# Decode attention with MLP on one core: last V tile in halves, slot addresses on 256-byte boundaries, early w2 rows, four stores

## Chip, cores and metric

One core of one Trainium2 chip. The metric is device time in microseconds (us) of an execution; medians of several runs are quoted. A profile adds one execution with a timeline; its span is about 1.5 us shorter than the timed number of the same kernel.

## The reference, cut to what matters

Batch 4, one query token, 32 heads of 128, a K and a V cache of 4096 positions: 8 MB for every tile (8 heads of one batch), 16 tiles of K and 16 of V, so 268 MB that are read once. Around them stand small projections.

```python
q = (layernorm(x) @ wq)                         # 4 x 640 -> 32 heads x 128
p = softmax(einsum("bhqd,bhkd->bhqk", q, k_cache) * Dh**-0.5)
h = x + einsum("bhqk,bhkd->bhqd", p, v_cache).reshape(4, 1, 4096) @ wo
t = layernorm(h) @ w1 + b1                      # 640 -> 1728
out = h + (t * tanh(softplus(t))) @ w2          # 1728 -> 640
```

## The kernel before

Three slots of 64 KB per partition take the K and V tiles. At the end wo and w1 come into slot B and w2 into slot A. One queue (SyncE) issues nearly all loads, in the order of this listing. TensorE does Q.K by folding products that VectorE made, then P.V, and in the tail a chain of small steps. `need` means "wait for"; the mark `("F", i, s)` says that part s of Q.K of tile i is folded, `("PV", i)` that P.V of tile i is done.

```python
SB0, SLOT0 = 16512, 229344 - 3 * SLOT * 2       # SLOT0 = 32736: 224 bytes past a multiple of 256
slot = {c: nc.alloc_sbuf_tensor_at(f"slot{c}", (P, SLOT), BF16,
        offset=SLOT0 + k * SLOT * 2).ap() for k, c in enumerate("ABC")}
...
def v_load(i):
    c = VS[i % N]
    load(sp, slot[c][:, :], tiles(A_v_cache, i), ("V", i), "V" + c)   # 128 rows of 64 KB
...
def sync_prog():
    ...                                          # K and V tiles; V of tile 15 is the last
    sp.need(("F", NT - 1, NS - 1))
    for q in range(NHG):                         # wo in four quarters of 1.3 MB
        load(sp, wo_sb[:, q, :, :], ..., ("wo", q), f"W{q}")
    for k, (c0, c1) in enumerate(zip(W1S, W1S[1:])):   # w1 in chunks 0-2 and 3-4
        load(sp, w1_sb[:, c0:c1, :], ..., ("w1", c0), f"W{NHG + k}")
    sp.need(("PV", NT - 2))
    load(sp, w2_tail[0:FT, :], B_w2[FM * P : F, :], "w2t", "WT")      # 64 rows, 80 KB
    for k, (j0, j1) in enumerate(zip(W2S, W2S[1:])):   # w2 in three parts
        load(sp, w2_sb[:, j0:j1, :], ..., ("w2", j0), f"W{NHG + 2 + k}")
    store(sp, 0); leave(sp, 0)                   # the other half of out goes by ScalarE's queue
...
def pv_mm(i):
    pe.need(("e", i, NS - 1), ("V", i))          # e: masked exponentials
    for u in range(nu):                          # 64 matmuls
        mm(pv[k * QD : (k + 1) * QD, :], e[...], t[:, u * 512 : (u + 1) * 512], ...)
...
def pe_tail():
    wo_mm(0); o_mm(NT - 1); l_mm(hg); wo_mm(1); a_mm(hg)   # wo_mm(k) needs wo quarter k and heads k
    ...
    wo_mm(2); wo_mm(3)
    ...                                          # layer norm, w1, mish, w2, o_bf
```

The softmax here doesn't subtract the row's maximum and nothing guards it: scores larger than these inputs give would overflow.

Of the kernel before, what the change touches and what calls it, by code (L numbers as in the profile page):

```python
# [14 lines left out]
class Prog:  # L15
# [38 lines left out]
    def do(self, fn, mark=None, sem=None, by=1):  # L54
# [5 lines left out]
                ins.then_inc(self.book.handles[sem], by)  # L60
        return ins


class Book:
    def __init__(self):
# [7 lines left out]
def kernel(  # L73
# [13 lines left out]
    nc = tc.nc  # L87
# [26 lines left out]

    book = Book()
    WSEM = ["WQ", "WT"] + [f"W{k}" for k in range(9)]
    for s in ["PE", "DV", "DVP", "DVA", "AC", "ACP", "PO", "KA", "KB", "VA", "VC", "X", "S", "OUT0", "OUT1", "FIN"] + WSEM:
        book.handles[s] = nc.alloc_semaphore(s)

    SB0, SLOT0 = 16512, 229344 - 3 * SLOT * 2  # L120
    at = [SB0]

    def sb(name, shape, dt, region=at, top=SLOT0):
# [17 lines left out]
    s_f = sb("s_f", (P, R), FP32)  # L141
    ex = sb("ex", (P, R), BF16)
    e = sb("e", (P, R, G), BF16)
    pv_sb = sb("pv_sb", (P, RQ, Dh), FP32)
    SW = 2 * BG - G
    selo = sb("selo", (P, RQ, SW), FP32)
    om = sb("om", (BG, G, Dh), BF16)
    rs = sb("rs", (P, N, NS), FP32)
    rs1 = sb("rs1", (P, N), FP32)
    rsm = sb("rsm", (P, N, G), FP32)  # L150
# [6 lines left out]
    delta = sb("delta", (BG, N), BF16)  # L157
    a_t = sb("a_t", (P, NHG, G, N), BF16)
    b1T = sb("b1T", (P, FC), BF16)
    eps = sb("eps", (P, 1), FP32)  # L160
    ones = sb("ones", (P, 1), FP32)

# [18 lines left out]
    w2_sb = slot["A"][:, 0 : FM * D].rearrange("p (j n) -> p j n", n=D)  # L181
    tail = [sA + FM * D * 2]
    topA = sA + SLOT * 2
    w2_tail = sb("w2_tail", (P, D), BF16, tail, topA)
    ones_d = sb("ones_d", (P, P), FP32, tail, topA)
    ident_f = sb("ident_f", (P, P), FP32, tail, topA)
    zeros = sb("zeros", (P, OC), BF16, tail, topA)
# [5 lines left out]
    std2 = sb("std2", (P, N), FP32, tail, topA)  # L193
    rstd = sb("rstd", (P, N), FP32, tail, topA)
    b1s = sb("b1s", (P, FC, N), FP32, tail, topA)
    ROW = QD // N
    spread = sb("spread", (P, 2 * DC + FC, N, ROW), BF16, tail, topA)
    h_hi, h_lo, act = (
        spread[:, j0:j1, :, :] for j0, j1 in ((0, DC), (DC, 2 * DC), (2 * DC, 2 * DC + FC))
    )  # L200
    h1 = sb("h1", (P, FC, N), FP32, tail, topA)
    ta = sb("ta", (P, FC, N), FP32, tail, topA)
    tb = sb("tb", (P, FC, N), FP32, tail, topA)
# [30 lines left out]
    po = Prog(nc.gpsimd, book)  # L234
    ac = Prog(nc.scalar, book)
    dv = Prog(nc.vector, book)
    pe = Prog(nc.tensor, book, take=["DVP", "DVA", "ACP", "VA", "VC"] + WSEM)

    def tiles(src, i):
        hg, b = divmod(i, N)  # L240
# [2 lines left out]
    def load(p, dst, src, key, sem):  # L243
        p.do(lambda: p.eng.dma_start(out=dst, in_=src), key, sem, 16)

    def store(p, h):
        c, n = CG // 2, D // 2
        p.need("o_bf")
        load(
            p, out_rows[:, h * n : (h + 1) * n].rearrange("b (k o) -> k b o", k=c),  # L250
            o_bf[h * P // 2 : (h + 1) * P // 2 : ROW, :], ("out", h), f"OUT{h}",
        )

    def leave(p, h):
        fin, o = book.handles["FIN"], book.handles[f"OUT{h}"]
        if p.live:
            p.eng.sem_inc(fin, 1)
            p.eng.wait_ge(o, 16).then_inc(o, -16)

    def clear():  # L260
        fin = book.handles["FIN"]
# [8 lines left out]

    def v_load(i):
        c = VS[i % N]
        load(sp, slot[c][:, :], tiles(A_v_cache, i), ("V", i), "V" + c)

    def first_loads():
        load(
            sp, slot["C"][:, 0 : DC * H * Dh], A_wq.rearrange("(p c) n -> p (c n)", c=DC), "wq", "WQ"
        )
        load(ac, x_bf[:, :], x_rows[:, :], "x", "X")
        k_load(0)  # L280
        k_load(1)

    def sync_prog():
        for hg in range(NHG):
            i = hg * N
            if hg:
                sp.need(("PV", i - 2))
                k_load(i)
                sp.need(("F", i - 1, NS - 1))
                k_load(i + 1)  # L290
            sp.need(("PV", i - 1) if hg else ("qb", NHG - 1))
            v_load(i)
            sp.need(("F", i, NS - 1))
            k_load(i + 2)
            sp.need(("PV", i))
            v_load(i + 1)
            sp.need(("F", i + 1, NS - 1))
            k_load(i + 3)
            sp.need(("F", i + 2, NS - 1))
            v_load(i + 2)  # L300
            sp.need(("PV", i + 1))
            v_load(i + 3)
        sp.need(("F", NT - 1, NS - 1))
        for q in range(NHG):
            load(
                sp, wo_sb[:, q, :, :],
                A_wo[q * QN : (q + 1) * QN, :].rearrange("(p j) n -> p j n", j=G), ("wo", q), f"W{q}",
            )
        w1_v = B_w1.rearrange("(p c) n -> p c n", c=DC)
        for k, (c0, c1) in enumerate(zip(W1S, W1S[1:])):  # L310
            load(sp, w1_sb[:, c0:c1, :], w1_v[:, c0:c1, :], ("w1", c0), f"W{NHG + k}")
        sp.need(("PV", NT - 2))
        load(sp, w2_tail[0:FT, :], B_w2[FM * P : F, :], "w2t", "WT")
        w2_v = B_w2[0 : FM * P, :].rearrange("(p j) n -> p j n", j=FM)
        for k, (j0, j1) in enumerate(zip(W2S, W2S[1:])):
            load(sp, w2_sb[:, j0:j1, :], w2_v[:, j0:j1, :], ("w2", j0), f"W{NHG + 2 + k}")
        store(sp, 0)
        leave(sp, 0)

    def pool_prog():  # L320
        g = nc.gpsimd
        po.do(lambda: g.memset(ident[:, :], 0.0), "id0", "PO")
        po.need("id0")
        po.do(
            lambda: g.affine_select(
                out=ident[:, :], in_=ident[:, :], compare_op=ALU.not_equal, fill=1.0, base=0,
                pattern=[[-1, P]], channel_multiplier=1,
            ),
            "ident", "PO",
        )  # L330
        po.do(lambda: g.memset(b1T[:, :], 0.0), "b1z", "PO")
        po.do(lambda: g.memset(lnT[:, :, :], 0.0), "lnz", "PO")
        po.do(lambda: g.memset(sel[:, :, :], 0.0), "selz", "PO")
        po.do(lambda: g.memset(selo[:, :, :], 0.0), "seloz", "PO")
        po.do(lambda: g.memset(ones[:, :], 1.0), "ones", "PO")
        po.need(("PV", NT - 2))
        po.do(lambda: g.memset(ones_d[:, :], 1.0 / D), "ones_d", "PO")
        po.do(lambda: g.memset(spread[:, :, :, :], 0.0), "spread", "PO")
        po.do(lambda: g.memset(zeros[:, :], 0.0), "zeros", "PO")
        po.do(lambda: g.tensor_copy(out=ident_f[:, :], in_=ident[:, :]), "ident_f", "PO")  # L340

# [80 lines left out]
    def dve_prog():  # L422
# [153 lines left out]
        for i in range(NT):  # L576
            hg, b = divmod(i, N)
            mult(i, 0)
            mult(i, 1)
            reduce(i, 0)  # L580
            mult(i, 2)
            if b == 0 and hg:
                norm(hg - 1)
            elif b == 0:
                dv.do(lambda: v.memset(om[:, :, :], 0.0), ("om", -1), DVP)
            reduce(i, 1)
            mult(i, 3)
            reduce(i, 2)
            if b == 0 and hg:
                heads(hg - 1)  # L590
            reduce(i, 3)
            for s in range(NS):
                mask(i, s)
            if b == N - 1:
                sums(hg)
# [12 lines left out]
        for k in range(2):  # L608
# [8 lines left out]
            if k == 0:  # L617
# [18 lines left out]
            ),  # L636
            "var", DV,
        )
        dv.do(lambda: v.tensor_copy(out=h_hi[:, :, :, 0], in_=st[:, 0, :, :]), "h_hi", DV)
        dv.need("std2", "b1b")  # L640
        dv.do(
            lambda: v.tensor_tensor(
# [6 lines left out]
        dv.need("h_hi")  # L649
        dv.do(  # L650
            lambda: v.tensor_tensor(
                out=h_lo[:, :, :, 0], in0=st[:, 0, :, :], in1=h_hi[:, :, :, 0], op=ALU.subtract
            ),
            "h_lo", DVP,
        )
# [26 lines left out]
        dv.need("tb3")  # L682
        dv.do(
            lambda: v.scalar_tensor_tensor(  # L684
                out=act[:, :, :, 0], in0=tb3[:, :, :], scalar=-0.5, in1=hm2[:, :, :],
                op0=ALU.add, op1=ALU.mult,
            ),
            "act", DVP,
# [83 lines left out]
    def pv_mm(i):  # L772
        t = slot[VS[i % N]][:, :]
        pe.need(("e", i, NS - 1), ("V", i))
        nu = R // RQ
        for u in range(nu):
            k = u % CG
            mm(
                pv[k * QD : (k + 1) * QD, :],
                e[:, u * RQ : (u + 1) * RQ, :].rearrange("p r g -> p (r g)"),  # L780
                t[:, u * 512 : (u + 1) * 512], u < CG, u >= nu - CG,
                ("PV", i) if u == nu - 1 else None,
            )
# [47 lines left out]
    def pe_tail():  # L831
# [49 lines left out]
        for part in (h_hi, h_lo):  # L881
            for k in range(CG):
                for c in range(DC):
                    mm(
                        y2_ps[k * QD : (k + 1) * QD, :].rearrange("b (m c) -> b c m", c=DC)[:, c, :],
                        part[:, c, :, :].rearrange("p n r -> p (n r)"), ident[:, k * QD : (k + 1) * QD], False, False,
                    )
        pe.need("act")

        def w2_mm(j):  # L890
            rows = P if j < FM else FT
            for k in range(CG):
                cs = slice(k * OC, (k + 1) * OC)
                done = j == FM - 1 and k == CG - 1
                mm(
                    y2_ps[k * QD : (k + 1) * QD, :],
                    act[0:rows, j, :, :].rearrange("p n r -> p (n r)"),
                    w2_sb[:, j, cs] if j < FM else w2_tail[0:FT, cs], False, j == FM - 1,
                    "y2" if done else None,
                )  # L900
# [73 lines left out]
```

## Time and profile before

| kernel before | value | where read |
|---|---|---|
| timed | 666.27 us (665.98 to 667.35) | four runs, those of the comparison below |
| span of the profile | 665.1 us | the page |
| K0 and K1 (the first two K tiles) in | 55.38 us | last packet of the load, DMA packet records |
| last byte of V | 636.63 us | same |
| last byte of wo, of w2 | 649.01, 660.28 us | same |
| end of o_bf, of the span | 663.05, 665.1 us | timeline |

A DMA packet here is the row of one partition: 128 packets of 64 KB make a K or V tile (4096 of them for 32 tiles in the trace of the kernel before).

First lines of the page of the kernel before. DMA gives the busy share of the 16 DMA engines in tenths, for 40 slices of the span; GB/s what they moved.

```profile
span 665.1 us, 5193 instructions
...
DMA  9999999999999999999999999999999999999996
GB/s 379 439 438 441 427 403 441 443 430 439 431 438 438 414 438 430 438 441 434 438 426 426 438 430 438 438 434 442 414 438 434 430 438 438 438 441 410 441 400 247
```

The DMA engines are busy throughout (9 tenths or more in 39 of 40 slices), so the body costs what its bytes cost. The same in two windows of the kernel before; the last three columns are granted TensorE clock, DMA share and GB/s:

```profile
core 0: us, PE busy (x) PEld busy (x) DVE busy (x) ACT busy (x) POOL busy (x), PEclk, DMA share, GB/s
100.00:600.00 500.00, 294.11 (x1798) 41.61 (x1018) 322.31 (x175) 25.65 (x117) 0.00 (x0) 0.79 1.00 433
```

433 GB/s in 500 us, at a DMA share of 1.00. Compute matters only after the last V byte. The chain of waits of the kernel before, in order of time (start, us, what):

```profile
637.16 0.04 issue
637.21 6.27 PE pv L695 x60
643.48 1.69 PE y_ps L695 x40
645.17 0.99 PE o_ps L695 x8
...
648.81 3.18 PE y_ps L695 x80
...
653.34 5.13 PE red L695 x72
...
660.04 0.42 DVE spread L684
...
660.50 2.20 PE red L695 x42
...
662.72 0.33 DVE o_bf L691
```

From P.V of the last tile on there is no DMA in this chain: compute alone sets the end. `y_ps` is wo, the first `red` is w1, the last one w2. 28.44 us pass from the last V byte to the end of the span.

### The profile page before, as it was taken

Reading aid. Unit: us, or ns where it says so; the run is one execution under the profiler, and the core shown is the slowest. Engines: PE = TensorE matmul, PEld = TensorE weight load, DVE = VectorE, ACT = ScalarE, POOL = GpSimd, SP = SyncE. Lnnn points to the kernel's source line nnn. Section 1 sums busy time; section 2 is a strip of 40 time slices with the busy share of each in tenths; the row PEclk is TensorE's granted clock in tenths of the full one; section 3 lists DMA queues with packets and bytes.
Section 4 is the critical chain, followed back from the end, with each engine's and each line's share of the span. In section 5 each row is a group of like instructions: output and inputs, shape, how many; then the busy total and the mean of one; then the engine's idle time right before and its main releaser. Section 6 shows DMA issues by size and latency. Waiting matters only on the chain. (4 is left out here: it accounts for less than half of the span.)

```text
span 665.1 us, 5193 instructions
## 1 busy us (share of the span) xinstructions
PE 396.6 (60%) x2747; PEld 80.1 (12%) x1787; DVE 407.2 (61%) x252; ACT 41.6 (6%) x158; POOL 3.3 (0%) x15
## 2 busy tenths in 40 slices
PE   0856658656317595848408395838335656655767
PEld 0600000101101010101100010100010001010147
DVE  1077988495048778677218798759207688948602
ACT  0200000000000000000000000000000000000011
POOL 1000000000000000000000000000000000000000
PEclk9768797979659796868657887879776769887865
DMA  9999999999999999999999999999999999999996
GB/s 379 439 438 441 427 403 441 443 430 439 431 438 438 414 438 430 438 441 434 438 426 426 438 430 438 438 434 442 414 438 434 430 438 438 438 441 410 441 400 247
DMA packets 6390, 283.50 MB, mean 426 GB/s; under 512 B 936, under 2 KB 1004, under 8 KB 1516
## 3 DMA queue, kind: packets, MB, share of 16 engines
q1 hardware_dynamic: 6138, 283.35, 98.9%
q8 instruction: 7, 0.11, 0.1%
q10 hardware_dynamic: 242, 0.01, 0.0%
q14 instruction: 3, 0.02, 0.0%
HBM read 283.35 MB, written 0.01 MB: 426 GB/s over the span
## 5 line engine op out<-in xcount | busy, mean ns | idle before, releaser
L503 DVE TENSOR_TENSOR slotA<-slotA,q_bc 128x8192 bf16<-128x8192 bf16 x32 | 140.7, 4416 | 109.0 <-DMA slotA<-in_A_k_cache_dram 109.0
L503 DVE TENSOR_TENSOR slotB<-slotB,q_bc 128x8192 bf16<-128x8192 bf16 x32 | 140.7, 4418 | 15.5 <-DMA slotB<-in_A_k_cache_dram 15.5
L514 DVE TENSOR_REDUCE s_f<-red 128x64 f32<-128x1024 f32 x64 | 78.0, 1219 | 99.6 <-PE red L705 99.5
L705 PE MATMUL red<-slotA,ident 128*128 128x512 bf16 x480 | 138.6, 453 | 0.0
L705 PE MATMUL red<-slotB,ident 128*128 128x512 bf16 x480 | 126.5, 423 | 0.0
L695 PE MATMUL red<-slotA,ident 128*128 128x512 bf16 x32 | 14.2, 445 | 120.2 <-PEq L49 120.2
L695 PE MATMUL pv<-slotC,e 128*32 128x512 bf16 x768 | 52.9, 438 | 40.7 <-PEq L49 40.7
L695 PE MATMUL red<-slotB,ident 128*128 128x512 bf16 x32 | 14.1, 441 | 86.3 <-PEq L49 86.3
L382 ACT ACTIVATE ex<-s_f 128x64 bf16<-128x64 f32 x64 | 16.4, 256 | 504.5 <-DVE s_f L514 504.5
L528 DVE TENSOR_TENSOR e<-ex,hmask 128x512 bf16<-128x512 bf16 x64 | 39.8, 684 | 0.0
L695 PEld LDWEIGHTS pv<-slotC,e 128*32 128x32 bf16 x768 | 22.8, 109 | 99.5 <-issue 86.3
L695 PEld LDWEIGHTS red<-slotA,ident 128*128 128x128 bf16 x32 | 3.1, 98 | 189.2 <-issue 189.2
L695 PEld LDWEIGHTS red<-slotB,ident 128*128 128x128 bf16 x32 | 3.2, 99 | 169.2 <-issue 169.2
L695 PEld LDWEIGHTS o_ps<-pv_sb,selo 128*32 128x32 f32 x136 | 13.5, 109 | 64.2 <-issue 64.2
L695 PE MATMUL o_ps<-pv_sb,selo 128*32 128x128 f32 x136 | 18.0, 276 | 0.0
L695 PE MATMUL pv<-slotA,e 128*32 128x512 bf16 x256 | 14.5, 380 | 0.9 <-PEq L49 0.9
L392 ACT COPY pv_sb<-pv 128x512 f32<-128x512 f32 x16 | 9.4, 585 | 74.1 <-PE pv L695 74.1
L382 ACT ACTIVATION_READ_ACCUMULATOR ex<-s_f 128x1 f32 x64 | 11.9, 187 | 0.0
L695 PE MATMUL red<-q_all,sel 32*128 32x128 bf16 x128 | 9.8, 264 | 0.8 <-PEq L49 0.8
L695 PEld LDWEIGHTS pv<-slotA,e 128*32 128x32 bf16 x256 | 6.9, 97 | 23.9 <-issue 18.2
L695 PEld LDWEIGHTS red<-q_all,sel 32*128 32x128 bf16 x128 | 9.5, 119 | 1.7 <-issue 1.7
L553 DVE RECIPROCAL rl<-misc 32x1 f32<-32x1 f32 x4 | 0.6, 151 | 14.8 <-PE misc L695 14.8
(95 smaller groups left out, 78.0 us busy)
## 6 DMA issues: line engine op xcount, KB each, us to landing
slotC<-in_A_wq_dram SPq DMA_DIRECT2D x1, 5120.0 KB, 15.4
slotB<-in_A_wo_dram SPq DMA_DIRECT2D x4, 1280.0 KB, 16.7
slotB<-in_B_w_dram SPq DMA_DIRECT2D x1, 1296.0 KB, 23.4
slotA<-in_B_w_dram SPq DMA_DIRECT2D x1, 960.0 KB, 27.2
slotB<-in_B_w_dram SPq DMA_DIRECT2D x1, 864.0 KB, 25.6
slotA<-in_B_w_dram SPq DMA_DIRECT2D x1, 800.0 KB, 28.5
slotA<-in_B_w_dram SPq DMA_DIRECT2D x1, 320.0 KB, 28.9
slotC<-in_A_v_cache_dram SPq DMA_DIRECT2D x12, 45.0
```

Of the source, the lines that this page charges most:

```text
L382: lambda: a.activation(out=ex[:, sl], in_=s_f[:, sl], func=ACT.Exp, scale=SCALE, accum_out=rs[:, b, s : s + 1],),
L392: lambda: a.copy(out=pv_sb[:, :, :].rearrange("p r d -> p (r d)"), in_=pv[:, :]),
L503: lambda: v.tensor_tensor(out=t, in0=t, in1=q_bc[:, hg, b, :].unsqueeze(1).to_broadcast([P, RS, Dh]), op=ALU.mult,),
L514: lambda: v.tensor_reduce(out=s_f[:, s * RS : (s + 1) * RS], in_=red[:, k : k + 2, :].rearrange("p k (r c) -> p (k r) c", c=CW), axis=AX.X ...
L528: lambda: v.tensor_tensor(out=e[:, sl, :], in0=ex[:, sl].unsqueeze(2).to_broadcast([P, RS, G]), in1=hmask[:, :].unsqueeze(1).to_broadcast( ...
L553: dv.do(lambda: v.reciprocal(out=rl[:, :], in_=l_ps), ("rl", hg), DV)
L695: lambda: nc.tensor.matmul(out_, lhsT=lhsT, rhs=rhs, start=start, stop=stop, skip_group_check=skip),
L705: return t.add_instruction(mybir.InstMatmult(name=nc.get_next_instruction_name(), engine=mybir.EngineType.PE, ins=[t.lower_ap(rhs), t.lowe ...
```

## The change

The intent: (1) load the last V tile in halves, so that half of its P.V runs while the second half is on its way; (2) put the slots on 256-byte boundaries; (3) load the last 64 rows of w2 at the start, off the tail; (4) give the output as four rows at a time, with dense h_hi, h_lo and act tiles in place of a zero-padded `spread` tile. The tile `om` shares the space of `pv_sb` to make the room.

```diff
-    SB0, SLOT0 = 16512, 229344 - 3 * SLOT * 2
+    SB0, SLOT0 = 16512, 127 * 256
...
-    om = sb("om", (BG, G, Dh), BF16)
+    om = nc.alloc_sbuf_tensor_at("om", (BG, G, Dh), BF16, offset=PV_AT).ap()
...
-    h_hi, h_lo, act = (spread[:, j0:j1, :, :] for ...)
+    h_hi = sb("h_hi", (P, DC, N), BF16, tail, topA)      # h_lo and act likewise
...
 def store(p, h):
-        load(p, out_rows[...].rearrange("b (k o) -> k b o", k=c), o_bf[... : ROW, :], ...)
+        for k in range(h, CG, 2):
+            load(p, out_rows[:, k * OC : (k + 1) * OC], o_bf[k * QD : k * QD + N, :], ...)
...
 def v_load(i):
-        load(sp, slot[c][:, :], tiles(A_v_cache, i), ("V", i), "V" + c)
+        n = SLOT // 2 if i == NT - 1 else SLOT
+        load(sp, slot[c][:, 0:n], src[:, 0:n], ("V", i), "V" + c)
+        if n < SLOT:
+            load(sp, slot[c][:, n:SLOT], src[:, n:SLOT], ("V2", i), "V2")
...
 def first_loads():
         load(ac, x_bf[:, :], x_rows[:, :], "x", "X")
+        load(ac, w2_tail[0:FT, :], B_w2[FM * P : F, :], "w2t", "WT")
...
         sp.need(("PV", NT - 2))
-        load(sp, w2_tail[0:FT, :], B_w2[FM * P : F, :], "w2t", "WT")
...
 def pv_mm(i):
+            if u == nu // 2 and i % N == N - 1:
+                pe.need(("V2", i))
```

So the w2 rows change their queue as well as their place: ScalarE's at the start, SyncE's at the end.

More of the change, by code (lines that the diff above doesn't have):

```diff
@@ L61, in do, with signal @@
         return ins
+    def signal(self, mark, sem, by):
+        self.count[sem] = self.count.get(sem, 0) + by
+        self.book.put(mark, sem, self.count[sem])
+        if self.live:
+            self.eng.sem_inc(self.book.handles[sem], by)
 class Book:
@@ L116 @@
     WSEM = ["WQ", "WT"] + [f"W{k}" for k in range(9)]
-    for s in ["PE", "DV", "DVP", "DVA", "AC", "ACP", "PO", "KA", "KB", "VA", "VC", "X", "S", "OUT0", "OUT1", "FIN"] + WSEM:
+    for s in ["PE", "DV", "DVP", "DVA", "AC", "ACP", "PO", "KA", "KB", "VA", "VC", "V2", "X", "S", "OUT0", "OUT1", "FIN"] + WSEM:
         book.handles[s] = nc.alloc_semaphore(s)
-    SB0, SLOT0 = 16512, 229344 - 3 * SLOT * 2
+    SB0, SLOT0 = 16512, 127 * 256
     at = [SB0]
@@ L143 @@
     e = sb("e", (P, R, G), BF16)
+    PV_AT = at[0]
     pv_sb = sb("pv_sb", (P, RQ, Dh), FP32)
@@ L159 @@
     b1T = sb("b1T", (P, FC), BF16)
+    w2_tail = sb("w2_tail", (P, D), BF16)
     eps = sb("eps", (P, 1), FP32)
@@ L183 @@
     topA = sA + SLOT * 2
-    w2_tail = sb("w2_tail", (P, D), BF16, tail, topA)
     ones_d = sb("ones_d", (P, P), FP32, tail, topA)
@@ L195 @@
     b1s = sb("b1s", (P, FC, N), FP32, tail, topA)
-    ROW = QD // N
-    spread = sb("spread", (P, 2 * DC + FC, N, ROW), BF16, tail, topA)
-    h_hi, h_lo, act = (
-        spread[:, j0:j1, :, :] for j0, j1 in ((0, DC), (DC, 2 * DC), (2 * DC, 2 * DC + FC))
-    )
+    h_hi = sb("h_hi", (P, DC, N), BF16, tail, topA)
+    h_lo = sb("h_lo", (P, DC, N), BF16, tail, topA)
+    act = sb("act", (P, FC, N), BF16, tail, topA)
     h1 = sb("h1", (P, FC, N), FP32, tail, topA)
@@ L236 @@
     dv = Prog(nc.vector, book)
-    pe = Prog(nc.tensor, book, take=["DVP", "DVA", "ACP", "VA", "VC"] + WSEM)
+    pe = Prog(nc.tensor, book, take=["DVP", "DVA", "ACP", "VA", "VC", "V2"] + WSEM)
     def tiles(src, i):
@@ L246, in store @@
     def store(p, h):
-        c, n = CG // 2, D // 2
         p.need("o_bf")
-        load(
-            p, out_rows[:, h * n : (h + 1) * n].rearrange("b (k o) -> k b o", k=c),
-            o_bf[h * P // 2 : (h + 1) * P // 2 : ROW, :], ("out", h), f"OUT{h}",
-        )
+        for k in range(h, CG, 2):
+            load(
+                p, out_rows[:, k * OC : (k + 1) * OC], o_bf[k * QD : k * QD + N, :],
+                ("out", k), f"OUT{h}",
+            )
     def leave(p, h):
@@ L257, in leave @@
             p.eng.sem_inc(fin, 1)
-            p.eng.wait_ge(o, 16).then_inc(o, -16)
+            p.eng.wait_ge(o, 32).then_inc(o, -32)
     def clear():
@@ L272, in v_load @@
         c = VS[i % N]
-        load(sp, slot[c][:, :], tiles(A_v_cache, i), ("V", i), "V" + c)
+        src = tiles(A_v_cache, i)
+        n = SLOT // 2 if i == NT - 1 else SLOT
+        load(sp, slot[c][:, 0:n], src[:, 0:n], ("V", i), "V" + c)
+        if n < SLOT:
+            load(sp, slot[c][:, n:SLOT], src[:, n:SLOT], ("V2", i), "V2")
+        elif i % N == N - 1:
+            sp.signal(("V2", i), "V2", 16)
     def first_loads():
@@ L337, in pool_prog @@
         po.do(lambda: g.memset(ones_d[:, :], 1.0 / D), "ones_d", "PO")
-        po.do(lambda: g.memset(spread[:, :, :, :], 0.0), "spread", "PO")
         po.do(lambda: g.memset(zeros[:, :], 0.0), "zeros", "PO")
@@ L584, in dve_prog @@
             elif b == 0:
+                dv.need(("O", -1))
                 dv.do(lambda: v.memset(om[:, :, :], 0.0), ("om", -1), DVP)
@@ L638, in dve_prog @@
         )
-        dv.do(lambda: v.tensor_copy(out=h_hi[:, :, :, 0], in_=st[:, 0, :, :]), "h_hi", DV)
+        dv.do(lambda: v.tensor_copy(out=h_hi[:, :, :], in_=st[:, 0, :, :]), "h_hi", DV)
         dv.need("std2", "b1b")
@@ L651, in dve_prog @@
             lambda: v.tensor_tensor(
-                out=h_lo[:, :, :, 0], in0=st[:, 0, :, :], in1=h_hi[:, :, :, 0], op=ALU.subtract
+                out=h_lo[:, :, :], in0=st[:, 0, :, :], in1=h_hi[:, :, :], op=ALU.subtract
             ),
@@ L684, in dve_prog @@
             lambda: v.scalar_tensor_tensor(
-                out=act[:, :, :, 0], in0=tb3[:, :, :], scalar=-0.5, in1=hm2[:, :, :],
+                out=act[:, :, :], in0=tb3[:, :, :], scalar=-0.5, in1=hm2[:, :, :],
                 op0=ALU.add, op1=ALU.mult,
@@ L884, in pe_tail @@
                     mm(
-                        y2_ps[k * QD : (k + 1) * QD, :].rearrange("b (m c) -> b c m", c=DC)[:, c, :],
-                        part[:, c, :, :].rearrange("p n r -> p (n r)"), ident[:, k * QD : (k + 1) * QD], False, False,
+                        y2_ps[k * QD : k * QD + N, :].rearrange("b (m c) -> b c m", c=DC)[:, c, :],
+                        part[:, c, :], ident[:, k * QD : (k + 1) * QD], False, False,
                     )
@@ L895, in w2_mm @@
                 mm(
-                    y2_ps[k * QD : (k + 1) * QD, :],
-                    act[0:rows, j, :, :].rearrange("p n r -> p (n r)"),
+                    y2_ps[k * QD : k * QD + N, :], act[0:rows, j, :],
                     w2_sb[:, j, cs] if j < FM else w2_tail[0:FT, cs], False, j == FM - 1,
```

## The prediction

> What bounds the kernel now. The page gives 283.5 MB in a span of 665.1 us, DMA at 9 tenths in 39 of 40 slices. In the trace's DMA packet records all 16 engines are occupied without a gap from 40 to 635 us, at a flat 433.3 GB/s; a 64 KB packet takes 2421 ns. [...] The body is transfer-bound; compute matters only in the tail. The last w2 piece lands at 660.8 us. The chain of waits shows a tail of compute alone: last V lands at 637.2, P.V (64 matmuls) 6.27 us, then wo, norm, w1, mish, w2, o_bf ending 663.05, stores, end 665.1: 4.3 us after the last load.
>
> The change:
> 1. Last V in halves. The first half lands about 9.7 us earlier (627.5), the masks e are ready at 631.1 (timeline), so half of P.V moves into a PE idle from 628.4 to 637.2. The chain after V shrinks by 3.1 us[...]: net 2.4, estimated. But w2 still lands at 660.8[...]. So the tail becomes bound by the w2 landing: about 1.3 of the 2.4 can be had, the rest turns into a wait for DMA. [...]
> 2. Slots on 256-byte boundaries; now they begin 224 bytes past one. [...]
> 3. Last rows of w2 beside x: same bytes, moved from 653-656 us, where the rate dips to 310-365 GB/s and engines then finish unevenly (658.8 to 660.8). Nearly a zero sum; up to 0.4 us.
> 4. Four 4-row stores: one issue of 0.65 us per queue becomes two of 0.33 to 0.43; packets came 1.8 us after issue. Within 0.2 us either way.
> 5. The spread tiles go: POOL memset of 0.74 us off the path, matmul count unchanged: nothing.
>
> Sum: 1.3 (tail) + 1.6 (alignment) + 0.2 (w2 rows) - 0.1 = 3.0 us. Predicted 663.2 us, range 661.7 to 665.0. Chances: faster by over 2% 0.01, within 2% 0.98, slower by over 2% 0.01.
>
> What would show it: 64 KB packets at 2410 to 2415 ns (alignment right) or still 2418 to 2421 (wrong); P.V of the last tile in two groups of 32, the first near 631; PE idle before the last w2 piece, and the end under 3.3 us after the last load (tail bound by w2); first output packet about 1.8 us after o_bf.
>
> What would make it wrong: alignment worth nothing (then about 664.8); the half clock stretching the tail so that compute still ends last; the engines' uneven finish growing; w2 rows beside x delaying wq and the first V load; slower completion of two stores per queue.

The 1.6 us for alignment is the author's estimate (the 2410 to 2415 ns named as its sign are from the same working), and the price of the packets that the halves add, 0.07 us, presumably the 0.1 taken off. Cut too is what made "net 2.4" of 3.1, a loss of the wo matmuls at half clock: by the clock records and timelines, 40 of them took 1.76 us at full clock (before, from 643.41 us) and 1.76 us at half (after, from 645.21 us). The 2.4 and the 1.3 are estimates.

## The result, and the profile after

The changed kernel: 664.39 us median (664.32 to 664.69, four runs), against 666.27 us of the kernel before. The ratio is 0.997, 95% interval 0.9952 to 0.9987: faster, but within 2%. A ratio here is the mean time of one kernel's fast runs over the mean of the other's of the same rounds, so not quite the ratio of the medians.

The page after:

```profile
span 662.8 us, 5202 instructions
...
DMA  9999999999999999999999999999999999999996
GB/s 381 440 435 415 424 440 439 437 439 436 412 439 439 435 431 439 439 427 427 443 431 435 435 443 431 423 439 428 435 439 443 431 423 439 431 431 439 425 414 275
```

And the window of the body after:

```profile
core 0: us, PE busy (x) PEld busy (x) DVE busy (x) ACT busy (x) POOL busy (x), PEclk, DMA share, GB/s
100.00:600.00 500.00, 296.55 (x1798) 41.40 (x1018) 323.98 (x175) 25.64 (x117) 0.00 (x0) 0.78 1.00 434
```

These views cannot show a quarter of a percent; 433 has become 434. The DMA packet records can. The chain of waits after:

```profile
625.33 22.87 DMA slotB<-in_A_wo_dram
648.20 0.05 issue
648.25 1.77 PE y_ps L706 x40
...
651.45 5.15 PE red L706 x72
...
658.17 0.23 DVE act L695
...
658.45 2.16 PE red L706 x56
...
660.63 0.32 DVE o_bf L702
```

A load has entered the chain: not w2, but wo. The timeline of TensorE after (start, us, instruction; in brackets the idle time before it and what ended it), the group that the first half of V now allows, the second half, and the four quarters of wo:

```profile
627.94 1.91 PE L706 MATMUL pv<-slotC,e 128*32 128x512 bf16 x32 [2.97 <-DVE rsm L554]
...
636.11 3.61 PE L706 MATMUL pv<-slotC,e 128*32 128x512 bf16 x32 [6.26 <-PEq L49]
...
639.65 1.76 PE L706 MATMUL y_ps<-a_t,slotB 128*128 128x4 bf16 x40
...
642.37 1.76 PE L706 MATMUL y_ps<-a_t,slotB 128*128 128x4 bf16 x40
...
645.21 1.76 PE L706 MATMUL y_ps<-a_t,slotB 128*128 128x4 bf16 x40
...
648.25 1.76 PE L706 MATMUL y_ps<-a_t,slotB 128*128 128x4 bf16 x40 [1.28 <-DMA slotB<-in_A_wo_dram]
```

The third quarter of wo now starts 9.54 us after the last V byte (645.21 less 635.67), where it took 12.01 us before (648.64 less 636.63), 2.5 us more; this is the line of the kernel before:

```profile
648.64 3.33 PE L695 MATMUL y_ps<-a_t,slotB 128*128 128x4 bf16 x80
```

Not all of that is the halves: in the changed kernel with V whole, told below, the third quarter starts 11.63 us after V (647.32, from its timeline, less 635.69). So the halves shorten the chain by 2.1 us. Then the fourth quarter waits 1.28 us for its load, which lands 12.2 to 12.4 us after V in every run here.

From the packet records of both (us; K0 and K1 are the first two tiles; the body is from there to the end of the 31st full tile):

| | before | after | difference |
|---|---|---|---|
| K0 and K1 in | 55.38 | 56.06 | +0.68 |
| body | 561.89 | 560.25 | -1.64 |
| last V byte | 636.63 | 635.67 | -0.96 |
| V to last wo byte | 12.38 | 12.22 | -0.16 |
| V to last w2 byte | 23.66 | 22.42 | -1.24 |
| last w2 byte to end of span | 4.78 | 4.70 | -0.08 |
| V to end of span | 28.44 | 27.12 | -1.32 |

The span is 2.3 us shorter in these two profiles: 1.0 by an earlier V, 1.3 in the tail.

### The profile page after: what moved, and what is told of

It reads as the page before. It is cut to its first block, busy times and chain, and to the rows that moved or that the text cites. A ratio compares the mean times of both kernels' runs of the same rounds, so it can differ in the third digit from the quotient of the medians.

```text
span 662.8 us, 5202 instructions
## 1 busy us (share of the span) xinstructions
PE 396.2 (60%) x2747; PEld 79.9 (12%) x1787; DVE 406.8 (61%) x252; ACT 41.5 (6%) x158; POOL 2.6 (0%) x14
## 5 line engine op out<-in xcount | busy, mean ns | idle before, releaser
L706 PE MATMUL red<-slotC,lnT 128*32 128x512 bf16 x40 | 4.5, 630 | 8.8 <-PEq L49 8.8
```

Source lines behind the costliest of these rows:

```text
L706: lambda: nc.tensor.matmul(out_, lhsT=lhsT, rhs=rhs, start=start, stop=stop, skip_group_check=skip),
```

## The experiments

Each kernel ran five rounds against the kernel before, on one chip per group of four. Every kernel gave a correct result. The differences are small, so the ranges of the five runs stand beside the medians; 0.3 us between medians is near the limit of what these runs tell.

### The changed kernel again

No edit.

> The changed kernel itself, for a common chip with the three beside it. Every theory: 0.997 of before (about 664.4 us), 64 KB packets at 2418 ns, PE waiting about 1.3 us for the last quarter of wo.

Measured: 664.29 us (664.12 to 664.62), before 666.33 us, ratio 0.9971. The result repeats; it is the base for the next three. In this profile K0 and K1 came in at 56.39, the body took 560.24 us.

### The slots back at the old addresses

```diff
-    SB0, SLOT0 = 16512, 127 * 256
+    SB0, SLOT0 = 16512, 127 * 256 + 224
```

> The changed kernel with the slots back at the old addresses (224 bytes past a 256-byte boundary). Theory A (alignment takes away packet jitter, worth about 1.3 us of the 64 KB packets and up to 1 us in the weights of the tail): median 64 KB packet back at 2421 ns, last V byte about 1.2 us later, time 1.5 to 2.0 us over the changed kernel, so most of the whole gain gone. Rival B (the gain comes from the V halves and the w2 rows; the jitter was a matter of the chip or of the run): packets stay at 2418 ns and the time within 0.3 us of the changed kernel.

Measured: 666.30 us (666.05 to 666.36), 2.0 us over the changed kernel and equal to the kernel before (ratio 0.9999). The last V byte came at 637.43 us against 636.00, 1.43 us later. So with the old addresses all other parts of the change together are worth nothing that shows, and theory A holds. The wait for wo stands in the tail as it does in the changed kernel; this is the chain of waits of this run:

```profile
627.13 23.19 DMA slotB<-in_A_wo_dram
650.32 0.04 issue
650.37 1.77 PE y_ps L706 x40
```

### Only the slot addresses changed in the kernel before

```diff
-    SB0, SLOT0 = 16512, 229344 - 3 * SLOT * 2
+    SB0, SLOT0 = 16512, 127 * 256
...
-    om = sb("om", (BG, G, Dh), BF16)
+    om = nc.alloc_sbuf_tensor_at("om", (BG, G, Dh), BF16, offset=PV_AT).ap()   # on pv_sb
...
+                dv.need(("O", -1))                 # pv_sb must be free before om is cleared
```

> The kernel before with the slot addresses alone changed to a 256-byte boundary (om shares the space of pv_sb to make the room). Theory A (alignment is nearly the whole gain): 64 KB packets at 2418 ns, last V byte 1.2 to 1.6 us earlier than in the kernel before, time 1.5 to 2.0 us shorter, so about 664.6 us. Rival (the gain needs the other parts too): under 1 us shorter.

Measured: 664.99 us (664.26 to 665.57), 1.4 us below 666.39 of the kernel before on that chip; ratio 0.9981, interval 0.9967 to 0.9995. The last V byte came at 635.15 us, 1.5 earlier than in the profile of before. A little under the expected 1.5 to 2.0 and over the rival's limit of 1; but the five runs spread over 1.3 us and the interval reaches from 0.3 to 2.2 us, so the time alone does not exclude the rival. The V byte, earlier by as much as it is later with the addresses undone (1.43), speaks for theory A: the addresses by themselves give most of the gain.

### Other offsets: 32, 64 and 128 bytes past the boundary

```diff
-    SB0, SLOT0 = 16512, 127 * 256
+    SB0, SLOT0 = 16512, 127 * 256 + 32        # also + 64, + 128
```

> The changed kernel with every slot 128 bytes past a 256-byte boundary. Theory A1 (a boundary of 256 bytes is what counts): packets and time as with 224 bytes past it, about 666.3 us. Theory A2 (64 or 128 bytes are enough): 2418 ns and about 664.3 us as the changed kernel.

> The changed kernel with every slot 64 bytes past a 256-byte boundary. A1 (256 counts): about 666.3 us. A2 (64 is enough): about 664.3 us. If 128 is enough and 64 is not, 128 past gives the fast time and this the slow one.

> The changed kernel with every slot 32 bytes past a 256-byte boundary. A1 and A2 (64 is enough): about 666.3 us, packets 2421 ns. Theory A3 (the amount of bytes below the start counts, 32 instead of 224): a cost of about a seventh, 664.5 us.

Measured: 665.78, 666.10 and 665.99 us for 128, 64 and 32 bytes, against 664.29 and 664.39 for the changed kernel (other chips; the kernel before took 666.39 on this one and 666.33 on that of the repeat). Neither 64 nor 128 bytes are enough, and 32 bytes past cost nearly as much as 224 in time: A1 holds, A2 and A3 fall. (The slots of the changed kernel begin at odd multiples of 256; the 2414.9 ns of the table were had without a larger boundary.) The packet records say it more sharply. The pace is the time from the end of tile 4 to the end of tile 31 (27 tiles, 216 packets of 64 KB on every engine), over 216; the next column is the share of 64 KB packets that last 2417 or 2418 ns, then their mean duration:

| slots past a multiple of 256 | pace, ns per packet | at 2417-2418 ns | mean ns |
|---|---|---|---|
| 0 (changed kernel, its repeat; V whole the same) | 2414.9 | 98% | 2419.7 |
| 0 (kernel before, slots alone) | 2415.3 | 97% | 2419.9 |
| 128 | 2418.8 | 23% | 2423.0 |
| 64 | 2419.2 | 16% | 2423.3 |
| 32 | 2421.1 | 0% | 2423.8 |
| 224 (changed kernel) | 2422.3 | 1% | 2423.8 |
| 224 (kernel before) | 2421.2 | 16% | 2424.1 |

(The last two columns of the first row are those of the repeat.) 2414.9 ns for 64 KB on each of 16 engines is 65536 * 16 / 2414.9 = 434.2 GB/s; 2422.3 is 432.9. Each of the four offsets run costs 4 to 7 ns for a packet. Packets that follow each other on an engine overlap a little (in the first row they last 2419.7 ns and end every 2414.9), so the pace and not the duration is what time is made of.

### The last V tile in one load

```diff
-        n = SLOT // 2 if i == NT - 1 else SLOT
+        n = SLOT
```

> The changed kernel with the last V tile in one load. Theory A (the tail is tied to the landing of the last quarter of wo, which hides all but about 1.3 us of what the halves save): P.V 6.3 us after V again, the wait for wo gone, time 1.0 to 1.5 us over the changed kernel. Rival B (the halves are worth nothing because the tail is bound by the loads anyway): within 0.3 us.

Measured: 664.55 us (664.34 to 664.84), 0.26 over the changed kernel, with ranges that overlap. That is the rival's expectation, and theory A's 1.0 to 1.5 us is refuted. In the profiles V to end of span is 27.65 us, against 27.12 and 27.09 with the halves. The chain of waits of this run shows where the rest went:

```profile
636.15 6.00 PE pv L706 x62
...
647.48 3.18 PE y_ps L706 x80
650.66 0.02 issue
650.68 0.19 DVE st L611
```

With V whole the wo matmuls end 14.97 us after V and nothing waits for a load; with the halves they end at 650.02, 14.35 us after V, because the last quarter of wo lands only 12.2 us after V. 2.1 us of shortened chain become 0.6 us.

### The last rows of w2 loaded late, as before

```diff
         load(ac, x_bf[:, :], x_rows[:, :], "x", "X")
-        load(ac, w2_tail[0:FT, :], B_w2[FM * P : F, :], "w2t", "WT")
...
         sp.need(("PV", NT - 2))
+        load(sp, w2_tail[0:FT, :], B_w2[FM * P : F, :], "w2t", "WT")
```

> The changed kernel with the last rows of w2 loaded where they were. Theory A (zero sum in bytes, and the tail waits for wo, which lies ahead of these rows in the queue): last V byte and wo land 0.2 to 0.4 us earlier than in the changed kernel because the start is freed of the 80 KB, time 0 to 0.4 us SHORTER. Rival B (the dip in rate at 653 to 656 us in the kernel before came from these rows, on half the partitions): w1 and w2 packets next to them slow again, last load up to 1 us later, time 0.2 to 0.8 us longer.

Measured: 664.04 us (663.62 to 664.30), 0.25 shorter than the changed kernel: theory A. Moving these rows to the start was a small loss. Over all profiles, K0 and K1 came in at 55.27 to 55.48 us where the rows were late (four kernels, the one before among them) and at 55.78 to 56.75 us where they were early (ten profiles). The 40 KB packets of wq, which run beside the early rows, took 1530 to 1608 ns in the median there and 1514 with the rows late. Part of the earlier start with late rows is lost again in the body, which took 560.25 us in the changed kernel and 560.76 here. Late, they do lengthen V to last w2 byte, 23.13 us against 22.42, and the first w2 packets beside them last 342 ns in the mean against 291, so rival B saw a true thing; but V to end of span stays at 27.10 us, since they stand behind wo in the queue and the chain does not wait for w2 (chain of waits of this run):

```profile
625.02 22.96 DMA slotB<-in_A_wo_dram
647.98 0.05 issue
648.03 1.77 PE y_ps L706 x40
```

The 80 KB would take 0.19 us at 434 GB/s; they cost more at either place. They go to partitions 0 to 63. No run here had the same bytes on all partitions, nor the same place with the other queue, so why they cost more was not shown.

### The last quarter of wo in halves

```diff
-            load(sp, wo_sb[:, q, :, :], ...("wo", q), f"W{q}")
+            for j0, j1 in (((0, 4), (4, 8)) if q == NHG - 1 else ((0, 8),)):
+                load(sp, wo_sb[:, q, j0:j1, :], ..., ("wo", q, j0), ...)
...
             for j in range(G):
+                if k == NHG - 1 and j == G // 2:
+                    pe.need(("wo", k, j))
```

> The changed kernel with the last quarter of wo loaded in two halves, each awaited by its own half of the matmuls. Theory C (after the change the tail waits for the landing of weights one after the other, wo first and w1 close behind it): the wait for wo (1.3 us) shrinks to about 0.4, but the first part of w1, which lands at about 651.4, takes over, so only 0.1 to 0.3 us shorter than the changed kernel. Rival D (only wo is late): 0.7 to 0.9 us shorter.

Measured: 664.51 us (664.13 to 665.04); the changed kernel had 664.29 on another chip, with 666.33 and 666.23 for the kernel before. No gain, so rival D is refuted; the 0.1 to 0.3 us of theory C do not show either. The timeline shows the next load taking over, w1, as theory C said:

```profile
646.50 3.43 PE L708 MATMUL y_ps<-a_t,slotB 128*128 128x4 bf16 x80
...
652.19 2.77 PE L708 MATMUL red<-cen,slotB 128*64 128x4 bf16 x42 [0.95 <-DMA slotB<-in_B_w_dram]
```

### w1 in three parts as well

```diff
-    W1S = (0, 3, DC)
+    W1S = (0, 2, 4, DC)                        # on top of the edit just told
```

> As wo_split, and w1 loaded in parts of two, two and one chunks instead of three and two. Theory C: the chain keeps up with the loads until w2; 0.9 to 1.5 us shorter than the changed kernel, about 663.1 us, with the end of the last matmul less than 1.3 us after the last load (2.5 us in the changed kernel). Rival D: no shorter than wo_split.

Measured: 664.23 us (664.12 to 664.49). V to end of span fell to 26.46 us, 0.6 below the changed kernel, and the wait for w1 is gone:

```profile
648.86 0.96 PE L708 MATMUL y_ps<-a_t,slotB 128*128 128x4 bf16 x20 [0.51 <-DMA slotB<-in_A_wo_dram]
...
651.19 3.77 PE L708 MATMUL red<-cen,slotB 128*64 128x4 bf16 x56
...
658.59 1.90 PE L708 MATMUL red<-slotA,act 128*4 128x160 bf16 x52
```

But the last matmul still ends 1.7 us after the last w2 byte (660.49 less 658.76), not under 1.3, and the timed gain is 0.1 us, not 0.9 to 1.5. A miss: wo still ends a wait of 0.51 us (the first line), and from there on no load does; the steps from wo through norm, w1 and mish to w2 are long enough by themselves. Part of the profile's 0.6 us is also hidden by the start: K0 and K1 came in 0.2 us later here than in the repeat of the changed kernel, a difference between runs.

### The same with V whole, and with the w2 rows late

```diff
-        n = SLOT // 2 if i == NT - 1 else SLOT       # tuned_v_whole
+        n = SLOT
```

> As tuned, with the last V tile in one load. Theory C (the halves of V were hidden by the weights that came late): here they are worth more than the 0.26 us that they were in the changed kernel: 1.0 to 1.6 us longer than tuned, near the time of the changed kernel with V whole (664.5 us). If the halves are worth little in themselves: within 0.4 us of tuned.

Measured: 664.57 us (664.23 to 664.95), 0.34 over the kernel with halves, not 1.0 to 1.6. In the profiles V to end of span differs by 1.0 us (27.44 against 26.46), but V came 0.63 us earlier in the profile with V whole, 0.53 of it already there when K1 had landed (56.06 against 56.59). Splitting the last tile cannot delay the first two; so this is the spread of the start, and 0.34 us is what the timed runs give.

```diff
-        load(ac, w2_tail[0:FT, :], B_w2[FM * P : F, :], "w2t", "WT")   # tuned_rows_late: moved
+        load(sp, w2_tail[0:FT, :], B_w2[FM * P : F, :], "w2t", "WT")   # behind w1, as before
```

> As tuned, with the last rows of w2 loaded at the end as in the kernel before. If the tail of tuned is bound by the last load: the same bytes are moved either way, last load within 0.2 us, time within 0.2 us of tuned. If the start is the worse place (half of the partitions beside wq): 0.2 to 0.4 us shorter than tuned.

Measured: 663.66 us (663.42 to 663.88), ratio 0.9958 to the kernel before (0.9944 to 0.9971), 0.57 below the kernel with the rows early on the same chip, more than either expectation gave. In the profiles V comes 0.65 us earlier with the rows late (635.60 against 636.25) and V to end of span takes 0.32 longer (26.78). It is the fastest version, 0.7 us below the changed kernel's 664.39, with ranges that do not meet. It leaves out one part of the change.

## Why the prediction was right or wrong

The time was right to 1.2 us (663.2 predicted, 664.39 measured, inside the range of 661.7 to 665.0), but the forecast gain was 3.0 us and the measured one 1.9, its tail term was five times too large in time, and its term for the w2 rows had the wrong sign. That the total stayed in the range is in part luck: alignment gave about the sum put down for it, but the sign named for it failed (2).

1. "The body is transfer-bound; compute matters only in the tail." Right: the pace of the packets (6.4 ns less on each of the 232 that an engine moves in the body) explains 1.5 of the 1.6 us between 561.89 and 560.25 us.

2. Alignment, 1.6 us in the sum, an estimate. Right in size, and mis-sized as a share: undoing it costs 2.0 us, doing it alone gives 1.4, so it is most of the result where it was counted as half. The sign that was named failed: "64 KB packets at 2410 to 2415 ns (alignment right) or still 2418 to 2421 (wrong)". The shortest packets are 2418 ns in both kernels. What alignment removed is the spread above it (16% of packets at 2417 or 2418 before, 98% after), and the pace fell by 6 to 7 ns. The cost does not follow the count of bytes past the boundary: 224 bytes cost 7.4 ns of pace, and 32 bytes, a seventh of them, 6.2 ns. What happens in the engine was not settled.

3. The halves: "net 2.4" of chain. Nearly right: 2.1 against V whole, 2.5 against the kernel before. "So the tail becomes bound by the w2 landing: about 1.3 of the 2.4 can be had" is the step that failed. The chain met a load sooner, the last quarter of wo 12.2 us after V, and the halves gave 0.26 us in time and 0.5 in the profile. "The end under 3.3 us after the last load" failed with it: 4.70 us. I compared the end of the chain with the last load and not every link with the load that it needs. A reading error came on top: the landings of 637.2 and 660.8 in the prediction are about 0.5 us late (the last packets ended at 636.63 and 660.28; their landing semaphores were complete at 637.07 and 660.75), and the 658.8 to 660.8 for the engines' uneven finish moves with them. The two groups of 32 came as foretold, the first at 627.94 us (630.49 in the repeat).

4. The tail of the profile is 1.3 us shorter all the same, the size that was forecast, but of other parts: that agreement is luck. The halves give 0.53 of it (against V whole). Another 0.12 belongs to the addresses: P.V starts 0.44 to 0.48 us after the last V byte in the nine profiles with aligned slots and 0.57 to 0.61 in the five without. Another 0.27 is P.V of the whole tile running faster in the V-whole run than in the kernel before (6.00 against 6.27 us), and 5.50 in the kernel before with slots alone. That is the clock that TensorE was granted: by the clock records 4.84, 5.37 and 3.82 us of the three ran at half clock. Counted at half, and added to the rest, they give 3.6 us each time, and P.V of an earlier tile took 3.64 us at full clock. When the half clock comes varies between runs, so I do not credit this to the change, and the 0.53 carries the same uncertainty. About 0.19 is `act` written densely (0.42 to 0.23 us in the chain), which the prediction set at "nothing". About 0.18 is from o_bf to the end of the span (2.02 to 1.84).

5. The stores: "within 0.2 us either way". Right by that 0.18 us. The 1.8 us from issue to first output packet, misread by the same 0.5 us, was 1.26 before and is 0.77 after.

6. The w2 rows: "nearly a zero sum", 0.2 us of gain put into the sum. Wrong in sign: 0.25 us lost in the changed kernel, 0.57 in the retuned one. They were taken from a place behind wo, where they were off the critical path, to one ahead of a body that is bound by transfers (DMA share 1.00 from 100 to 600 us). That the place and not the queue did it is argued, not shown.

Taken out one at a time from the changed kernel, the parts add up: 2.0 us from the addresses, 0.26 from the halves, 0.25 lost by the rows, about nothing left for the rest, against 1.9 to 2.0 measured. That the kernel with all parts except the addresses equals the kernel before (0.9999) says the same in one run. Put in first, the addresses give 1.4 us and leave 0.6 to the rest; these runs are too few to say whether the parts help each other or the 0.6 is spread.

What stays open: why slots 32 to 224 bytes past a 256-byte boundary slow a packet, and why 64 and 128 bytes cost less in pace (3.9 to 4.3 ns) than 32 and 224 (6.2 to 7.4). Also why K0 and K1 come in with a spread of up to 1 us from run to run when the w2 rows are early.

## What to carry to other kernels

When the DMA engines are saturated (a DMA share of 1.00 over 500 us here), look at the pace of packets over hundreds of microseconds, not at one packet or a page in tenths: here the address of three buffers was worth 0.2 to 0.3%, more than all the reordering in the tail. When a compute chain in the tail is shortened, ask of every link when the load it needs lands; here the first late load, the last quarter of wo, took 1.5 of the 2.1 us, and it was not the last load. Before moving bytes off a tail, see whether the tail waits for them: here it did not, and ahead of a body bound by transfers they cost more than their own time (0.25 to 0.57 us for rows of 0.19 us).
